# Causal scores in 64x64 array tiles, the state's products moved ahead of them, and the work around them reordered, in a gated linear attention followed by a routed FFN

## The chip, the cores and the metric

One core of a Trainium2 chip runs the whole program. The metric is device time in microseconds of one launch; smaller is better. The engines are PE (matmul) with its weight loads PEld, DVE (vector), ACT (scalar), POOL (GpSimd) and SP, which here only issues DMAs. SP issues to the hardware DMA queue, POOL issues the indirect (gather and scatter) DMAs to the software queue.

## The reference

All data is float32. Attention has batch B=4, H=8 heads, S=768 steps, head size D=48; its result becomes the rows x of an FFN with E=8 experts of which each row takes its two best.

```python
f = 1 / (1 + exp(-f_logit))
for t in range(S):
    state = f[:, :, t, :, None] * state + einsum('bhd,bhe->bhde', k[:, :, t], v[:, :, t])
    y[:, :, t] = einsum('bhd,bhde->bhe', q[:, :, t], state)
x = y as (B*S, H*D) = (3072, 384)
noisy = x @ w_gate + log1p(exp(x @ w_noise)) * noise
top2, weights = two largest of noisy, softmax over the two
out[row] = sum over the two e of weight_e * (relu(x[row] @ w1[e]) @ w2[e])    # w1: 384x1024, w2: 1024x384
```

## The kernel before

**Steps.** The attention is cut into 24 steps: n = c*B + b, with c one of 6 chunks of C=128 time steps and b the batch. A step handles all 8 heads, as HP=4 pairs (`hp`); the two heads of a pair (`par`) lie on partitions 0 to 63 and 64 to 127, each padded from 48 to DP=64.

**Stages of a step.** `forget` transposes f on PE and takes its log on ACT. `summed` is a running sum on DVE (a tensor-tensor scan, L554). `decays` makes P and Q, two exponentials of the sum, on ACT. `scaled` transposes q and k on PE; DVE multiplies them into qP (L566) and kQ (L568). `scores` transposes kQ back (kp, L574; not in the last chunk), multiplies kQ by qP on PE into a two-bank PSUM tile `sc` (L580), and DVE multiplies that by the lower-triangle mask `causal` into A (L583). `output` multiplies A by v on PE (y, L598), makes the state's increment ds from kn and v (L604), adds the state's part, state by qP, to y (L609; not in the first chunk), has ACT copy y (yT, L613) and ds (dss, L618) out of PSUM, and POOL computes the new state from dss, the old state and P (mid L625, st L626). `features` multiplies yT by a constant matrix (xp, L633) that brings x into row order and gives the router's logits; ACT copies the rows (xs, L638), which SP stores to `x_rows` in DRAM at the next `scaled` (L639).

**Order.** An outer loop over i runs from -3 to 25. In each pass every stage handles its own step n = i - lag, in a written order; between the stages small pieces of other work are dropped in. `slot` counts the stages run. From the line `first` on, each engine's instructions keep the order in which they are traced. In the last passes, stages that have run out of steps are left out.

**Loads.** `load` (L528) brings f, q, k and v of a step, 192 KB each, in one DMA of 192-byte runs. They go into rings of 5, 4, 4 and 6 buffers. POOL clamps f two passes ahead of its use (L534); for the first three steps DVE does it.

**Routing.** After every fourth step `route(c)` works out the two experts of a chunk's rows, one small group of instructions a slot. Its end gives 8 `put`s: each a scatter by POOL (L710) of 128 list entries to the `lists` tensor in DRAM, and a small memset (L719). One put is issued every third slot.

**The FFN's beginning.** When the puts of the first three chunks (24 of them) have been issued, the generator `first_loads` begins: after some slots SP fetches the first list (`slots<-lists`, L815), POOL gathers the rows that it names (`xg<-x_rows`, L826, in two halves), and PE transposes them (`turned`, xgp, L862). After that, pieces of expert 0's first layer (hp, L914) are put between the last stages of the attention. The rest of the FFN follows as one stream, most of it matmuls of L914, L939 and L1021.

**Zeros.** `out` is first filled with zeros, since the FFN's results are added to it: 24 DMAs of 192 KB on SP (L1254), twelve of them one at a time at the outputs of steps 5 to 16, twelve in the FFN. `lists` is filled from the tile `empty` at step 5 (L1309). SP also issues the first experts' weights in parts of 384 KB (L841, L844), from step 17 on.

**PSUM.** Six banks (`one_bank`) are taken in turn by all products but the scores.

Of the kernel before, what the change touches and what calls it, by code (L numbers as in the profile page):

```python
# [10 lines left out]
F32 = mybir.dt.float32  # L11
# [320 lines left out]
def kernel(  # L332
# [89 lines left out]
        turns.append(turns.pop(0))  # L422
        return turns[-1].tile([128, 512], F32, tag="one", name=name)

    def two_banks(name):
        return ps2.tile([128, 2, 512], F32, tag="two", name=name)


    ident = const.tile([128, 128], F32, tag="ident", name="ident")
# [23 lines left out]
    def counting(name, pattern, base=0, by_partition=0):  # L453
# [9 lines left out]
    over_of = counting("over_of", [[QS, NI]], base=3 * 256)  # L463
    block = counting("block", [[1, NI]])

    causal = const.tile([128, 128], F32, tag="causal", name="causal")
    nc.gpsimd.affine_select(out=causal, in_=ones, compare_op=ALU.is_ge, fill=0.0, base=0,
                            pattern=[[1, 128]], channel_multiplier=-1)
# [5 lines left out]
    LR = E * N + 256  # L474
    x_rows = tc.dram_tile([N, DM], F32, name="x_rows")
    lists = tc.dram_tile([LR, 4], U32, name="lists")
    empty = const.tile([128, LR // 128, 4], U32, tag="empty", name="empty")

    cap = [const.tile([128, HP, C], F32, tag=f"cap{i}", name=f"cap{i}") for i in range(2)]
    for i in range(2):  # L480
# [44 lines left out]
    def load(nm, n):  # L525
        c, b = n // B, n % B
        if n < NCH * B:
            nc.sync.dma_start(out=pads[nm][n % RING[nm]][:, :, 0:D],  # L528
                              in_={"f": f_logit, "q": q, "k": k, "v": v}[nm][b, :, c * C:(c + 1) * C, :].rearrange("h t d -> t h d"))

    def clamp(n, engine=nc.gpsimd):
        if n < NCH * B:
# [31 lines left out]
    def scaled(n):  # L564
        qP[n] = wk.tile([128, HP * C], F32, tag="qP", name=f"qP_{n}", bufs=3)
        nc.vector.tensor_tensor(qP[n], transposed("q", n), P[n], ALU.mult)  # L566
        kQ[n] = wk.tile([128, HP * C], F32, tag="kQ", name=f"kQ_{n}")
        nc.vector.tensor_tensor(kQ[n], transposed("k", n), Q[n], ALU.mult)  # L568

    def scores(n):  # L570
        if n // B < NCH - 1:
            kp = one_bank(f"kp_{n}")
            for hp in range(HP):
                nc.tensor.transpose(kp[:, cols(hp)], kQ[n][:, cols(hp)], ident)  # L574
            kn[n] = wk.tile([C, H, DP], F32, tag="kn", name=f"kn_{n}")
            nc.scalar.copy(kn[n].rearrange("t h d -> t (h d)"), kp)
        sc = two_banks(f"sc_{n}")
        for hp in range(HP):
            for par in range(2):
                nc.tensor.matmul(sc[:, par, cols(hp)], lhsT=kQ[n][rows(par), cols(hp)],  # L580
                                 rhs=qP[n][rows(par), cols(hp)], start=True, stop=True)
        A[n] = wk.tile([C, 2, HP * C], F32, tag="A", name=f"A_{n}")
        nc.vector.tensor_tensor(A[n].rearrange("j r (a i) -> j (r a) i", i=C), sc.rearrange("j r (a i) -> j (r a) i", i=C),  # L583
                                causal.unsqueeze(1).broadcast_to((C, H, C)), ALU.mult)

    def output(n):
        c, b = n // B, n % B
        vt = pads["v"][n % RING["v"]]


        y = [one_bank(f"y{odd}_{n}") for odd in range(2)]

        def at(hp, par):
            return y[hp % 2][rows(par ^ hp % 2), cols(hp // 2)]

        for hp in range(HP):
            for par in range(2):
                nc.tensor.matmul(at(hp, par), lhsT=vt[:, 2 * hp + par, :], rhs=A[n][:, par, cols(hp)],  # L598
                                 start=(hp < 2), stop=(c == 0 and hp >= HP - 2))
        if c < NCH - 1:  # L600
            ds = one_bank(f"ds_{n}")
            for hp in range(HP):
                for par in range(2):
                    nc.tensor.matmul(ds[rows(par), hp * DP:(hp + 1) * DP], lhsT=kn[n][:, 2 * hp + par, :],  # L604
                                     rhs=vt[:, 2 * hp + par, :], start=True, stop=True)
        if c:
            for hp in range(HP):
                for par in range(2):
                    nc.tensor.matmul(at(hp, par), lhsT=state[b][rows(par), hp, :],  # L609
                                     rhs=qP[n][rows(par), cols(hp)], start=False, stop=(hp >= HP - 2))  # L610
        yT[n] = wk.tile([128, 2, HP // 2 * C], F32, tag="yT", name=f"yT_{n}")
        for odd in range(2):
            nc.scalar.copy(yT[n][:, odd, :], y[odd][:, 0:HP // 2 * C])  # L613
        if c == NCH - 1:
            return

        dsv = wk.tile([128, HP, DP], F32, tag="ds", name=f"dss_{n}")
        nc.scalar.copy(dsv, ds[:, 0:HP * DP].rearrange("d (a e) -> d a e", e=DP))  # L618
        end = P[n].rearrange("d (a t) -> d a t", t=C)[:, :, C - 1:C].broadcast_to((128, HP, DP))
        new = wk.tile([128, HP, DP], F32, tag=f"st{b}", name=f"st_{n}")  # L620
        if c == 0:
            nc.gpsimd.tensor_tensor(new, dsv, end, ALU.mult)
        else:
            mid = wk.tile([128, HP, DP], F32, tag="mid", name=f"mid_{n}")
            nc.gpsimd.tensor_tensor(mid, dsv, state[b], ALU.add)  # L625
            nc.gpsimd.tensor_tensor(new, mid, end, ALU.mult)  # L626
        state[b] = new
# [631 lines left out]
    def first_loads():  # L1259
        while n_routed < HALF or len(n_put) < HALF * B * 2:  # L1260
            yield
        for _ in range(3):
            yield
        for what, p, pause in (("fetch", 1, 5), ("first", 0, 3), ("second", 0, 1), ("fetch", 2, 4), ("turned", 0, 0),
                               ("first", 1, 3), ("second", 1, 1), ("fetch", 3, 1)):
            if what == "fetch":
                ahead(what, p)
            elif what == "first":
                gather(p, (0,))
            elif what == "second":  # L1270
# [12 lines left out]
    slot = n_routed = n_first = 0  # L1283
    pieces = chain.from_iterable(((k, i) for i, _ in enumerate(first_layer(k) if k < NE else first_of_two(k))) for k in range(len(items)))
    for i in range(-3, NS + 2):
        for stage, lag in ((forget, -3), (scaled, -1), (scores, 0), (summed, -2), (output, 1), (decays, -2), (features, 2)):
            n = i - lag
            if not 0 <= n < NS:
                continue
# [128 lines left out]
```

## Time and profile before

| | us |
|---|---|
| median of 3 runs (657.47 to 659.05) | 657.95 |
| profiled execution: its own time | 658.33 |
| profiled execution: its span | 656.6 |
| busy in the span: PE / DVE / POOL / ACT | 635.6 / 442.6 / 272.6 / 254.0 |
| one pass in the middle of the attention (score products at 61.6, then 67.62) | 6.0 |
| first score product of step 0 / of step 22 | 12.76 / 138.84 |
| first piece of expert 0 | 149.27 |

The span runs from the first to the last instruction; 1.7 us of the execution lie outside of it. The last steps of the attention lie among the first pieces of expert 0 and end at about 170 us. A record of a matmul lasts longer than the array is taken by it, since the records overlap; what a group costs PE is read from the start of one group to the start of the next. Each matmul of these float32 operands has two records, so the 8 score products of a step are 16.

### The profile page before, as it was taken

The page shows a single profiled execution, that of the slowest core. Times are in us where ns is not written, and L with a number is a line of the kernel's source. Part 1 is how long each engine was busy: PE and PEld are TensorE (multiplying, and loading weights), DVE is VectorE, ACT ScalarE, POOL GpSimd, SP SyncE. Part 2 cuts the span into 40 slices and gives each one's busy share as a digit, 9 for nine tenths or more (in the row PEclk, how much of TensorE's full clock was granted, in tenths as well). Part 3 has the DMA queues.
Part 4 walks back from the last instruction along what each step waited for, and adds up shares of the span by engine and source line. Part 5 has one row for each costly group of instructions (what it writes and reads, how often), then busy time and mean ns, then how long its engine had stood idle before and what let it go on. Part 6 is the DMA issues. An engine that isn't in the chain of part 4 may idle for free.

```text
span 656.6 us, 12905 instructions
## 1 busy us (share of the span) xinstructions
PE 635.6 (97%) x4883; PEld 549.1 (84%) x4883; DVE 442.6 (67%) x993; ACT 254.0 (39%) x603; POOL 272.6 (42%) x300
## 2 busy tenths in 40 slices
PE   7999999979999999999999999999999999999991
PEld 7999999968999999989758965995698579889891
DVE  7777877854476577677657575666666666766751
ACT  5876776732222234233332233223332332232320
POOL 8633999853187531352502450334035114413021
PEclk9999999999999999999999999999999999999996
DMA  9999988982998423368707560925275246601122
GB/s 192 195 221 213 199 188 185 205 248 31 321 311 189 66 37 96 70 192 288 197 25 252 93 193 0 317 42 175 72 245 124 65 146 187 180 2 25 23 25 29
DMA packets 153897, 96.31 MB, mean 147 GB/s; under 512 B 115600, under 2 KB 146320, under 8 KB 153824
## 3 DMA queue, kind: packets, MB, share of 16 engines
q1 hardware_dynamic: 141648, 76.12, 42.1%
q0 software_dynamic: 12176, 19.25, 15.0%
q8 instruction: 41, 0.67, 0.4%
q14 instruction: 32, 0.26, 0.1%
HBM read 75.97 MB, written 19.62 MB: 146 GB/s over the span
## 4 chain that ended last, share of the span: by engine, by line
PE 92%; DMA 4%; DVE 1%; POOL 1%; issue 1%; SPq 0%; POOLq 0%; DVEq 0%
PE y L1021 32%; PE P L939 8%; PE hp L914 6%; PE W L939 5%; PE Z L939 5%; PE V L939 5%; PE X L939 5%; PE y L598 4%; PE xp L633 3%; PE sc L580 3%; PE xgp L862 2%; PE y L609 2%; PE fp L540 1%; PE kp L540 1%; PE ds L604 1%; PE kp L574 1%
## 5 line engine op out<-in xcount | busy, mean ns | idle before, releaser
L1030 POOL DMA_INDIRECT out_dram<-ys,slots x48 | 81.2, 1691 | 178.1 <-ACT ys L1088 144.6
L1021 PE MATMUL y<-qk_all,f_all 128*128 128x192 f32 x576 | 105.2, 327 | 0.0
L1021 PEld LDWEIGHTS y<-qk_all,f_all 128*128 128x128 f32 x576 | 93.3, 190 | 0.3 <-DVE f_all L1003 0.3
L826 POOL DMA_INDIRECT xg<-x_rows,slots x48 | 54.2, 1130 | 19.9 <-issue 11.1
L710 POOL DMA_INDIRECT lists<-entry,sloti x48 | 55.4, 1153 | 10.6 <-issue 9.3
L1021 PE MATMUL y<-w,hs_b 128*128 128x192 f32 x320 | 59.1, 328 | 0.0
L1021 PEld LDWEIGHTS y<-w,hs_b 128*128 128x128 f32 x320 | 52.9, 190 | 0.9
L1162 POOL DMA_INDIRECT out_dram<-ys_q,slots_q x5 | 8.6, 1713 | 104.6 <-DVE ys_q L1160 104.6
L914 PE MATMUL hp<-xt_a,w 128*128 128x256 f32 x192 | 43.7, 382 | 0.0
L975 ACT ACTIVATE hs_b<-hs_b 128x256 f32<-128x256 f32 (+1 forms) x32 | 15.1, 470 | 71.7 <-DVE hs_b L955 71.7
L914 PEld LDWEIGHTS hp<-xt_a,w 128*128 128x128 f32 x192 | 35.8, 190 | 4.8 <-issue 0.2
L939 PE MATMUL X<-xt_a,w 128*128 128x256 f32 (+1 forms) x128 | 39.7, 432 | 0.0
L939 PE MATMUL Z<-xt_b,v_all 128*128 128x256 f32 (+1 forms) x128 | 39.7, 432 | 0.0
L1080 DVE TENSOR_TENSOR ys<-P,y 128x192 f32<-128x192 f32 x24 | 8.5, 354 | 43.1 <-PE y L1021 29.8
L583 DVE TENSOR_TENSOR A<-sc,causal 128x1024 f32<-128x1024 f32 x24 | 29.3, 1222 | 10.0 <-PE sc L580 9.1
L1088 ACT ACTIVATE ys<-ys,slots 128x384 f32<-128x384 f32 x24 | 14.8, 615 | 55.1 <-DVE ys L1087 55.1
L955 DVE TENSOR_TENSOR hs_b<-hs_a,X 128x256 f32<-128x256 f32 (+1 forms) x32 | 15.6, 487 | 29.9 <-PE X L939 29.8
L1021 PE MATMUL y<-w,f_all 128*128 128x192 f32 x192 | 35.1, 326 | 0.0
L939 PEld LDWEIGHTS Z<-xt_b,v_all 128*128 128x128 f32 x128 | 24.3, 190 | 10.1
L939 PEld LDWEIGHTS X<-xt_a,w 128*128 128x128 f32 x128 | 24.3, 190 | 10.1
L955 DVE TENSOR_TENSOR hs_a<-hs_a,P 128x256 f32<-128x256 f32 (+1 forms) x64 | 31.1, 485 | 1.5
L1021 PEld LDWEIGHTS y<-w,f_all 128*128 128x128 f32 x192 | 31.9, 190 | 0.0
(199 smaller groups left out, 1437.4 us busy)
## 6 DMA issues: line engine op xcount, KB each, us to landing
w<-in_moe_w_dram SPq DMA_DIRECT2D x16, 1536.0 KB, 8.5
w_q<-in_moe_w_dram SPq DMA_DIRECT2D x10, 1536.0 KB
w<-in_moe_w_dram SPq DMA_DIRECT2D x16, 384.0 KB, 5.3
f_all<-in_f_logit_dram SPq DMA_DIRECT2D x24, 192.0 KB, 3.4
qk_all<-in_q_dram SPq DMA_DIRECT2D x24, 192.0 KB, 4.5
qk_all<-in_k_dram SPq DMA_DIRECT2D x24, 192.0 KB, 4.6
v_all<-in_v_dram SPq DMA_DIRECT2D x24, 192.0 KB, 5.3
x_rows<-xs SPq DMA_DIRECT2D x24, 192.0 KB, 5.8
```

The lines of the kernel that those rows point to most:

```text
L580: nc.tensor.matmul(sc[:, par, cols(hp)], lhsT=kQ[n][rows(par), cols(hp)], rhs=qP[n][rows(par), cols(hp)], start=True, stop=True)
L583: nc.vector.tensor_tensor(A[n].rearrange("j r (a i) -> j (r a) i", i=C), sc.rearrange("j r (a i) -> j (r a) i", i=C), causal.unsqueeze(1). ...
L598: nc.tensor.matmul(at(hp, par), lhsT=vt[:, 2 * hp + par, :], rhs=A[n][:, par, cols(hp)], start=(hp < 2), stop=(c == 0 and hp >= HP - 2))
L633: nc.tensor.matmul(xp[:, hp, :], lhsT=yT[n][:, hp % 2, cols(hp // 2)], rhs=w_rt[:, hp, :], start=True, stop=True)
L710: into = nc.gpsimd.indirect_dma_start(out=lists, out_offset=bass.IndirectOffsetOnAxis(ap=sloti[:, r, b:b + 1], axis=0), in_=entry[:, c, b, ...
L826: nc.gpsimd.indirect_dma_start(out=xg[p][:, s, :], out_offset=None, in_=x_rows[0:HALF * B * C] if p < NE else x_rows, in_offset=bass.Indir ...
L914: nc.tensor.matmul(hp[:, o, :], lhsT=w1[home(k)][:, i, (fo + o) * 128:(fo + o + 1) * 128], rhs=xt_a[:, i, k % 2 * 256:(k % 2 + 1) * 256], ...
L939: nc.tensor.matmul(to, lhsT=x, rhs=y, start=start, stop=stop)
L955: nc.vector.tensor_tensor(to, x, y, ALU.add)
L975: nc.scalar.activation(c(1, 1), c(1, 1), AF.Relu)
L1021: nc.tensor.matmul(P[name], lhsT=x[:, o, :], rhs=y[:, o, :], start=(o == 0), stop=(o == FH - 1))
L1030: into = nc.gpsimd.indirect_dma_start(out=out, out_offset=bass.IndirectOffsetOnAxis(ap=slots[p][:, s, 2:3], axis=0), in_=ys[s], in_offset= ...
```

## The change

It does nine things.

1. The scores go to one PSUM tile for the whole attention, `sc_all`, which DVE fills with zeros once at the start. Each pair's product is made in two parts: the earlier 64 rows of keys (T=64) with all 128 queries, and the later 64 with the later 64 queries. The quarter that the mask would clear is not written. A product now has 64 partitions of kQ, 64 columns of it, and 128 or 64 columns of qP: 16 matmuls a step instead of 8.
2. In heads 4 to 7 the two halves of the keys are swapped: kQ is written with them exchanged, so DVE makes kQ in two instructions; v of these heads is loaded likewise, so a load of v is three DMAs. The pairs are taken in the order 0, 2, 1, 3.
3. The mask `causal` is a tile of four pairs instead of one, made by six POOL instructions instead of one.
4. `empty` is half as large, and `lists` is filled from it in two DMAs.
5. The state's part of y (`from_state`) is issued in the next `scores`, between the kp transposes and the score products; it starts the accumulation, and A by v ends it.
6. `features` stands ahead of `decays` in a pass.
7. While the third chunk's routing is the last begun, a put is issued every second slot instead of every third.
8. `first_loads` waits 7 slots instead of 3; its later pauses are 4, 2, 1, 6 where they were 5, 3, 1, 4.
9. The attention's twelve zeros go out two at a time at the outputs of steps 17 to 22.

```diff
+    sc_all = ps2.tile([128, 2, 512], F32, tag="two", name="sc_all")
+    nc.vector.memset(sc_all, 0.0)
...
+    T = C // 2
+    causal = const.tile([128, HP, 128], F32, tag="causal", name="causal")
+    for hp in range(HP):
+        for base, n in ((0, 128),) if hp < HP // 2 else ((T, 128), (-T, T)):
+            nc.gpsimd.affine_select(out=causal[0:n, hp], in_=(causal[0:n, hp] if n == T else ones), ...
...
-    empty = const.tile([128, LR // 128, 4], U32, tag="empty", name="empty")
+    empty = const.tile([128, LR // 256, 4], U32, tag="empty", name="empty")
...
+            nc.sync.dma_start(out=to[:, 0:H // 2], in_=rows_in[0:H // 2].rearrange("h t d -> t h d"))
+            for half in range(2):
+                nc.sync.dma_start(out=to[half * T:(half + 1) * T, H // 2:],
+                                  in_=rows_in[H // 2:, (1 - half) * T:(2 - half) * T].rearrange("h t d -> t h d"))
...
-        nc.vector.tensor_tensor(kQ[n], transposed("k", n), Q[n], ALU.mult)
+        kt = transposed("k", n)
+        for far_ in range(2):
+            out_, x, y = (z.rearrange("d (o a s t) -> d o a s t", o=2, s=2, t=T)[:, far_] for z in (kQ[n], kt, Q[n]))
+            nc.vector.tensor_tensor(out_[:, :, ::-1, :] if far_ else out_, x, y, ALU.mult)
...
-        for hp in range(HP):
-            for par in range(2):
-                nc.tensor.matmul(sc[:, par, cols(hp)], lhsT=kQ[n][rows(par), cols(hp)],
-                                 rhs=qP[n][rows(par), cols(hp)], start=True, stop=True)
+        if n:
+            from_state(n - 1)
+        for hp in (0, 2, 1, 3):
+            for late_rows in range(2):
+                half = hp // 2 ^ late_rows
+                for par in range(2):
+                    nc.tensor.matmul(sc_all[half * T:(half + 1) * T, par, hp * C + late_rows * T:(hp + 1) * C],
+                                     lhsT=kQ[n][rows(par), hp * C + half * T:hp * C + (half + 1) * T],
+                                     rhs=qP[n][rows(par), hp * C + late_rows * T:(hp + 1) * C], start=True, stop=True)
...
+    def from_state(n):
+        y_of[n] = [one_bank(f"y{odd}_{n}") for odd in range(2)]
+        if n // B:
+            for hp in range(HP):
+                for par in range(2):
+                    nc.tensor.matmul(place(n, hp, par), lhsT=state[n % B][rows(par), hp, :],
+                                     rhs=qP[n][rows(par), cols(hp)], start=(hp < 2), stop=False)
...
-        for _ in range(3):
+        for _ in range(7):
             yield
-        for what, p, pause in (("fetch", 1, 5), ("first", 0, 3), ("second", 0, 1), ("fetch", 2, 4), ("turned", 0, 0),
+        for what, p, pause in (("fetch", 1, 4), ("first", 0, 2), ("second", 0, 1), ("fetch", 2, 6), ("turned", 0, 0),
...
-        for stage, lag in ((forget, -3), (scaled, -1), (scores, 0), (summed, -2), (output, 1), (decays, -2), (features, 2)):
+        for stage, lag in ((forget, -3), (scaled, -1), (scores, 0), (summed, -2), (output, 1), (features, 2), (decays, -2)):
...
-                    nc.sync.dma_start(out=lists.rearrange("(p r) w -> p r w", p=128), in_=empty)
+                    for part in range(2):
+                        nc.sync.dma_start(out=lists.rearrange("(g p r) w -> g p r w", g=2, p=128)[part], in_=empty)
...
-                if 5 <= n < 5 + NS // 2:
-                    zeros(1)
+                if 17 <= n < 17 + NS // 4:
+                    zeros(2)
...
-            if puts and slot % 3 == 0:
+            if puts and slot % (2 if n_routed == HALF else 3) == 0:
```

More of the change, by code (lines that the diff above doesn't have):

```diff
@@ L423, in one_bank @@
         return turns[-1].tile([128, 512], F32, tag="one", name=name)
-    def two_banks(name):
-        return ps2.tile([128, 2, 512], F32, tag="two", name=name)
+    sc_all = ps2.tile([128, 2, 512], F32, tag="two", name="sc_all")
+    nc.vector.memset(sc_all, 0.0)
     ident = const.tile([128, 128], F32, tag="ident", name="ident")
@@ L464 @@
     block = counting("block", [[1, NI]])
-    causal = const.tile([128, 128], F32, tag="causal", name="causal")
-    nc.gpsimd.affine_select(out=causal, in_=ones, compare_op=ALU.is_ge, fill=0.0, base=0,
-                            pattern=[[1, 128]], channel_multiplier=-1)
+    T = C // 2
+    causal = const.tile([128, HP, 128], F32, tag="causal", name="causal")
+    for hp in range(HP):
+        for base, n in ((0, 128),) if hp < HP // 2 else ((T, 128), (-T, T)):
+            nc.gpsimd.affine_select(out=causal[0:n, hp], in_=(causal[0:n, hp] if n == T else ones), compare_op=ALU.is_ge, fill=0.0,
+                                    base=base, pattern=[[1, 128]], channel_multiplier=-1)
     earlier = const.tile([128, 128], F32, tag="earlier", name="earlier")
@@ L527, in load @@
         if n < NCH * B:
-            nc.sync.dma_start(out=pads[nm][n % RING[nm]][:, :, 0:D],
-                              in_={"f": f_logit, "q": q, "k": k, "v": v}[nm][b, :, c * C:(c + 1) * C, :].rearrange("h t d -> t h d"))
+            to = pads[nm][n % RING[nm]][:, :, 0:D]
+            rows_in = {"f": f_logit, "q": q, "k": k, "v": v}[nm][b, :, c * C:(c + 1) * C, :]
+            if nm != "v":
+                nc.sync.dma_start(out=to, in_=rows_in.rearrange("h t d -> t h d"))
+                return
+            nc.sync.dma_start(out=to[:, 0:H // 2], in_=rows_in[0:H // 2].rearrange("h t d -> t h d"))
+            for half in range(2):
+                nc.sync.dma_start(out=to[half * T:(half + 1) * T, H // 2:],
+                                  in_=rows_in[H // 2:, (1 - half) * T:(2 - half) * T].rearrange("h t d -> t h d"))
     def clamp(n, engine=nc.gpsimd):
@@ L576, in scores, with place @@
             nc.scalar.copy(kn[n].rearrange("t h d -> t (h d)"), kp)
-        sc = two_banks(f"sc_{n}")
-        for hp in range(HP):
-            for par in range(2):
-                nc.tensor.matmul(sc[:, par, cols(hp)], lhsT=kQ[n][rows(par), cols(hp)],
-                                 rhs=qP[n][rows(par), cols(hp)], start=True, stop=True)
-        A[n] = wk.tile([C, 2, HP * C], F32, tag="A", name=f"A_{n}")
-        nc.vector.tensor_tensor(A[n].rearrange("j r (a i) -> j (r a) i", i=C), sc.rearrange("j r (a i) -> j (r a) i", i=C),
-                                causal.unsqueeze(1).broadcast_to((C, H, C)), ALU.mult)
+        if n:
[7 more added lines that the diff above has]
+                                     rhs=qP[n][rows(par), hp * C + late_rows * T:(hp + 1) * C], start=True, stop=True)
+        A[n] = wk.tile([C, 2, HP * C], F32, tag="A", name=f"A_{n}")
+        nc.vector.tensor_tensor(A[n], sc_all, causal.rearrange("j a i -> j (a i)").unsqueeze(1).broadcast_to((C, 2, HP * C)), ALU.mult)
+    y_of = {}
+    def place(n, hp, par):
+        return y_of[n][hp % 2][rows(par ^ hp % 2), cols(hp // 2)]
+    def from_state(n):
[5 more added lines that the diff above has]
+                                     rhs=qP[n][rows(par), cols(hp)], start=(hp < 2), stop=False)
     def output(n):
@@ L588, in output @@
         vt = pads["v"][n % RING["v"]]
-        y = [one_bank(f"y{odd}_{n}") for odd in range(2)]
-        def at(hp, par):
-            return y[hp % 2][rows(par ^ hp % 2), cols(hp // 2)]
+        if n not in y_of:
+            from_state(n)
+        y = y_of[n]
         for hp in range(HP):
             for par in range(2):
-                nc.tensor.matmul(at(hp, par), lhsT=vt[:, 2 * hp + par, :], rhs=A[n][:, par, cols(hp)],
-                                 start=(hp < 2), stop=(c == 0 and hp >= HP - 2))
+                nc.tensor.matmul(place(n, hp, par), lhsT=vt[:, 2 * hp + par, :], rhs=A[n][:, par, cols(hp)],
+                                 start=(c == 0 and hp < 2), stop=(hp >= HP - 2))
         if c < NCH - 1:
@@ L605, in output @@
                                      rhs=vt[:, 2 * hp + par, :], start=True, stop=True)
[L606 to L610, printed above, removed]
         yT[n] = wk.tile([128, 2, HP // 2 * C], F32, tag="yT", name=f"yT_{n}")
```

## The prediction

> **What bounds the kernel now.** I read the page first, then the groups by line, PE's and POOL's timelines in the attention, the waits and the chain.
>
> The page's slices and the chain, shares by engine:
>
> ```profile
> PE   7999999979999999999999999999999999999991
> POOL 8633999853187531352502450334035114413021
> ...
> PE 92%; DMA 4%; DVE 1%; POOL 1%; issue 1%; SPq 0%; POOLq 0%; DVEq 0%
> ```
>
> PE is full but for the start and the ninth slice; POOL is full in slices 5 to 7, about 66 to 115 us. PE's timeline, one pass:
>
> ```profile
> 66.65 0.60 PE L540 MATMUL kp<-ident,qk_all 128*128 128x128 f32 x4
> 67.09 0.60 PE L574 MATMUL kp<-ident,kQ 128*128 128x128 f32 x4
> 67.62 1.16 PE L580 MATMUL sc<-qP,kQ 64*128 64x128 f32 x16
> 68.71 1.09 PE L598 MATMUL y<-A,v_all 128*64 128x128 f32 x16
> 69.63 0.64 PE L604 MATMUL ds<-v_all,kn 128*64 128x64 f32 x16
> 70.20 0.67 PE L609 MATMUL y<-qP,st 64*64 64x128 f32 x16
> 70.80 1.15 PE L633 MATMUL xp<-w_rt,yT 128*128 128x112 f32 x8
> ```
>
> From start to start: scores 1.09, y 0.92, ds 0.57, state 0.60, xp 0.98; with 1.84 for the four transposes 6.0 us a pass, without idle time: PE sets the pace. The ninth slice, in the chain of waits from 126 us:
>
> ```profile
> 128.97 6.08 DMA lists<-entry,sloti
> ...
> 135.06 1.73 DMA slots<-lists
> ...
> 137.61 6.70 DMA xg<-x_rows,slots
> ...
> 144.35 0.79 PE xgp L862 x3
> 145.13 1.91 PE y L598 x16
> ```
>
> PE finishes the scores of step 22 at 139.95 and waits in front of xgp for the gathered rows until 144.35; by the windows its clock is then at half for 3.4 us (0.53 in 144.35 to 148.00). The loss is 4.35 + 1.7 us. The chain starts at the 24th put. When does POOL issue that?
>
> ```profile
> 125.58 1.68 POOL L710 DMA_INDIRECT lists<-entry,sloti  x1 [0.22 <-issue]
> 127.27 0.09 POOL L719 MEMSET spacer<- 1x1 f32 x1
> 127.32 0.73 POOL L625 TENSOR_TENSOR mid<-dss,st 128x256 f32<-128x256 f32 x1
> 128.13 0.68 POOL L626 TENSOR_TENSOR st<-mid,P 128x256 f32<-128x256 f32 x1
> 128.97 1.01 POOL L710 DMA_INDIRECT lists<-entry,sloti  x1 [0.16 <-issue]
> ```
>
> POOL has no gap over 0.3 us before it; from 66 to 130 us it is busy 58.9 of 64 us and the rest is 0.15 to 0.2 us ahead of each put. Put 16, traced at the scores of step 16 (104.2), runs at 108.88. So POOL is behind its order of work, and the 24th put goes out when POOL's work is done. After 145 us PE has no idle time: what the attention gains or loses reaches the end.
>
> **What the Trainium skill says.** "TensorEngine Tiling (Array Packing)", Tiling Modes: 64x64 gives four tiles that work independently, and a change of mode drains the array. The trace agrees with both: the records of the state's products (64x64) start four together every 0.109 us, and around each change of shape 0.15 to 0.2 us are lost. The same page, Performance Considerations, says that a matmul has about 60 cycles of overhead and one column costs as much as 60; ds (64 columns) starts a pair every 0.058 us against 0.109 for 128, so 64 columns still pay half here. "GPSIMD Engine Reference", Specifications: POOL shares its SBUF port with DVE's instructions of two SBUF inputs. The puts that meet DVE's scan take 1.7 to 1.9 us instead of 1.0 (that at 125.58, scan from 125.28 to 126.49). "DMA: Bandwidth & Descriptors", SWDGE vs HWDGE vs iDMA: an engine takes turns between the software and the hardware queue; no view here shows the shares.
>
> **The change, part by part.**
>
> *Scores.* Before: 8 pairs of records, every 0.111 us: 0.89. After, each of the four tiles gets four records of 128 and four of 64 columns, and the order 0, 2, 1, 3 gives both column halves the same. 128 columns cost 0.109 (state). A 64x64 product of 64 columns is not in the trace: between 0.058 (ds) and 0.109; I take ds. 4 x 0.109 + 4 x 0.058 = 0.67 (to 0.87): gain 0.22 (0.02 to 0.22).
>
> *State ahead.* Shapes run full, scores, y/ds, state, full: four changes. Leftovers from the records: into scores 0.19, scores to y 0.15, ds to state 0.15, state to xp 0.18. After: full to state 0.15, none to the scores, 0.15, 0.18. Gain 0.19, in steps with a state. A pass then takes 6.0 - 0.41 = 5.6 us.
>
> *Start.* DVE's zeroing of 1024 columns: six memsets of 128 columns take 0.87 us at 4.63, so 1.16. DVE idles 0.59 before its first clamp, which the chain runs through: +0.5 (0 to 1.2). POOL makes five more masks (0.25 each) and four memsets half as long (-0.7): its first clamp, 7.94 to 9.74, moves by 0.4, and its reader starts at 10.81: nothing.
>
> *DVE.* kQ in two instructions: +0.1 a pass (128x512 takes 0.68, 128x256 about 0.42). A stays 1024 wide. DVE is busy 51.8 of 64 us and waits for the scores (7.2 us in 14 waits); that covers it.
>
> *Loads.* v adds two issues of 0.4 us a step to SP, a zero less saves 0.5 to 0.7; bytes stay. v is loaded three steps ahead, so nothing. The second DMA of `lists`: 0.4 us of SP once, at step 5, long before the first put.
>
> *Features ahead of decays.* On ACT the rows' copy (0.49) goes before P and Q; but y is now complete after A by v and its copy no longer waits for ds and the state (1.1 us), so P is not later. The copy also frees the bank that y takes earlier. Cost nothing.
>
> *The 24th put.* POOL's full stretch begins with the state update of step 8, at 65.9, which waits for dss. Up to there PE gains 5 x 0.22 + 5 x 0.41 - 0.5 = 2.65, counted at xp (64.79 to 62.1); y and ds end there, dss ends at 62.75 instead of 65.8, the update starts at 62.8. POOL's work from there to the 24th put is 63.1 us. The update of step 18 falls behind the put (-1.65), and a shorter pass puts one more scan in the way (+0.7). So 62.8 + 63.1 - 1.65 + 0.7 = **124.9**, 4.1 earlier. Every second slot brings nothing: POOL is late already. It also ends up further behind PE: st of step 16 ends at 116.87 and P of step 20, which takes its buffer (four), starts at 121.0; that margin of 4 us goes, and ACT may wait up to 2 us at steps 16 to 19. PE's following idle time covers that.
>
> *The rows.* From put to rows 15.4 us: 124.9 + 15.4 = **140.3**. The later fetch (7 slots) reaches SP near 123 and still waits for the puts.
>
> *PE's arrival.* xp in the pass of step 21, 136.89, moves to 129.3 (2.65 + 12 x 0.41). Then xp 0.98, transposes 0.97, state 0.44, scores 0.82 with the change of shape, y of step 21 0.92: PE stands before xgp at 133.5 and idles 6.8 us. The clock halves as before.
>
> *Sum.* The rows come 4.05 earlier; y and state of step 21, 0.92 + 0.60, are done ahead of the wait instead of behind it; step 23 gains 0.41. Total **-6.0 us**. The profiled execution (658.33, span 656.6 and 1.7 around it) becomes 652.3; it stands 0.4 over the median, 657.95, so I forecast **652.0**. A measurement tells 0.3%, 2 us, from no change.
>
> **Rivals.**
>
> *The chain is shorter than I add it up, and the wait goes.* For it: puts take 1.0 us without a scan, the packets of the puts at 119.47 and 124.26 were through 3.3 us later against 5.5 for the 24th, and without zeros at steps 5 to 16 the queues are emptier. Then PE's own gain shows: 7.6 + 0.41 + 0.41 (steps to 21, 22, 23) and the 6.05 us of the stall: 643.5; half of it 648. Against: POOL's work does not shrink with DMA traffic.
>
> *The zeros take the gather's place.* Ten zeros are issued before the rows arrive; 128 packets of 1536 bytes at 67 ns over 16 engines are 0.54 us each, 5.4 us. If all of it lies in the chain: 657.4, no change. Against: SP, stuck on the fetch, leaves the queues empty; DMA's share was 0.64 from 130 to 140.
>
> *Slower: the column halves take turns.* Place: the score products. The scores now run only two tiles at a time, and a row pair shares its columns; if that stays so, 8 x 0.109 + 8 x (0.058 to 0.109) = 1.34 to 1.74 instead of 0.89. Over 22 steps, less the change of shape, PE arrives 7 to 16 us later, the wait is gone, and the end is 1.3 to 10.8 later: 659 to 669, 664 in the middle. It decides from a score block of 1.3 us. Against: the state's products start four at a time.
>
> That the change doesn't do what it says I see no way for, except the put rate, dealt with above.
>
> **How the numbers follow.** Forecast 0.53 (649 to 655 by itself: the chain 3 us shorter or longer); wait gone or halved 0.22; zeros in the way 0.12; slower 0.13. Faster: 0.53 + 0.22 + 0.05 of the zeros' case = 0.80; same 0.07; slower 0.13. The range leaves out the slower case and the end of the fastest: 645.0 to 657.5.
>
> **What would show it.** Score groups 0.7 to 0.8 us from start to start with four records together; passes of 5.6 us; the 24th put near 125, rows near 140, PE idle 6 to 7 us before xgp, with POOL again without gaps. Wrong if PE does not wait there, if a score block is over 1.1 us, or if put to rows is not 14 to 17 us.

## The result, and the profile after

The changed kernel takes **677.59 us** (675.14 to 678.51) against 658.5 us for the kernel before beside it: a ratio of 1.0281, 95% interval 1.0245 to 1.0317. The forecast was 652.0. The profiled execution has a span of 676.2 us, 19.6 more than before. Every ratio here is taken over fast executions alone, so it is not quite the quotient of the medians beside it (in the second group below, where the kernel before scattered from 664 to 680 us, the two differ by up to 0.8%).

The page's slices of the kernel after, in tenths of busy time (the granted clock in the third line, the DMA engines' share in the fourth):

```profile
PE   8999988963999999999999999999999999999990
POOL 7544677816047634151441351235034214413021
PEclk9999998995999999999999999999999999999996
DMA  9887777799199533264753761646093337602112
```

Where PE had only the ninth slice short of full, it now has gaps from the sixth slice on and almost stands still in the tenth. POOL is nowhere full in slices 4 to 7. The DMA share falls there to 0.7 to 0.8; by the windows from 62 to 122 us it is 0.77 after and 0.90 before, at 151 and 198 GB/s. PE, POOL and the DMA engines all do less per us: something else must hold them back.

PE's own part came out as planned. PE's timeline, one undisturbed pass:

```profile
68.29 0.67 PE L612 MATMUL y<-qP,st 64*64 64x128 f32 x16
68.78 0.85 PE L596 MATMUL sc_all<-qP,kQ 64*64 64x128 f32 x32
69.55 1.09 PE L625 MATMUL y<-A,v_all 128*64 128x128 f32 x16
```

State 0.49, scores 0.77 from start to start; passes 5 to 8 start 5.57 us apart. But from the scores of step 9 (63.0) to those of step 17 (117.8) a pass takes 6.85 us, 6.16 before. The chain of waits shows through what (start, us, what):

```profile
81.59 4.64 DMA x_rows<-xs
...
89.61 4.69 DMA x_rows<-xs
...
95.69 7.53 DMA x_rows<-xs
...
150.83 4.23 DMA slots<-lists
...
158.61 6.48 DMA xg<-x_rows,slots
...
165.22 0.87 PE xgp L884 x3
```

Stores of rows, which the chain of before did not hold, stand in it from step 12 to step 15. ACT's timeline says how (in brackets the idle time ahead of an instruction and what ended it):

```profile
94.37 0.48 ACT L660 COPY xs<-xp 128x384 f32<-128x384 f32 x1 [3.75 <-DMA x_rows<-xs]
94.75 0.63 ACT L569 ACTIVATE P<-L 128x512 f32<-128x512 f32 x1
95.28 0.62 ACT L571 ACTIVATE Q<-L 128x512 f32<-128x512 f32 x1
```

xs has three buffers. Its copy waits until the store of three steps ago has landed, and P and Q of a later step stand behind it on ACT; DVE then waits for P (18.8 us in 17 waits from 12 to 175 us). Why are the stores late? The queue that issues them, SP's timeline:

```profile
83.51 1.00 SPq L536 DMA_DIRECT2D v_all<-in_v_dram  x1
84.56 1.27 SPq L538 DMA_DIRECT2D v_all<-in_v_dram  x2
85.88 0.61 SPq L508 DMA_DIRECT2D noise<-in_moe_noise_dram  x1
86.59 0.44 SPq L534 DMA_DIRECT2D f_all<-in_f_logit_dram  x1
87.13 0.53 SPq L534 DMA_DIRECT2D qk_all<-in_q_dram  x1
87.76 1.76 SPq L534 DMA_DIRECT2D qk_all<-in_k_dram  x1
89.61 1.89 SPq L661 DMA_DIRECT2D x_rows<-xs  x1
91.54 0.43 SPq L536 DMA_DIRECT2D v_all<-in_v_dram  x1
```

SP has no gap much over 0.1 us; the store at 89.61 lies behind all the loads. v's two half loads (L538) take 1.27 us together in nearly every step. Adding up SP's issues from the scores of step 9 to those of step 17 gives 5.62 us of 6.16 a step before and 6.34 of 6.85 after. This share says little: it is 88 to 97% in every kernel traced here, since the same kind of issue lasts longer in some places than in others. What tells is how late SP is. Here are a copy of rows and its store, and a load of k and its first use on PE, first before, then after (the 24 of each are matched in order):

```profile
66.83 0.50 ACT L638 COPY xs<-xp 128x384 f32<-128x384 f32 x1
...
70.40 0.59 SPq L639 DMA_DIRECT2D x_rows<-xs  x1
...
93.55 2.25 SPq L528 DMA_DIRECT2D qk_all<-in_k_dram  x1
...
109.96 0.60 PE L540 MATMUL kp<-ident,qk_all 128*128 128x128 f32 x4
```

```profile
80.56 0.48 ACT L660 COPY xs<-xp 128x384 f32<-128x384 f32 x1 [2.39 <-DVE lg L658]
...
95.69 1.34 SPq L661 DMA_DIRECT2D x_rows<-xs  x1
```

The load of k at 87.76, above, is used here, and PE waits for it:

```profile
93.55 0.63 PE L550 MATMUL kp<-ident,qk_all 128*128 128x128 f32 x4 [0.33 <-DMA qk_all<-in_k_dram]
```

From step 9 to 17 a store follows the end of its copy by 2.6 to 4.7 us before and by 12.4 to 16.7 after, so these stores do not wait for their copies: SP is some 10 us, about a step and a half, later than before. And k is loaded 15.1 to 16.8 us ahead of its use before, 5.8 to 8.1 after: the three steps of look-ahead are almost gone.

The fetch of the slots, in front of the FFN, is late too. First SP before the change, then after it, around the first fetch of the slots:

```profile
129.12 0.41 SPq L639 DMA_DIRECT2D x_rows<-xs  x1
135.06 0.37 SPq L815 DMA_DIRECT2D slots<-lists  x1
```

```profile
148.81 1.27 SPq L538 DMA_DIRECT2D v_all<-in_v_dram  x2
150.13 0.60 SPq L863 DMA_DIRECT2D w<-in_moe_w_dram  x1
150.83 0.43 SPq L837 DMA_DIRECT2D slots<-lists  x1
151.30 0.94 SPq L1276 DMA_DIRECT2D out_dram<-zero  x2
```

Before, SP stood idle from 129.5 until the 24th put had landed. After, that put is issued at 131.77, and SP comes to the fetch only 19.06 us later, straight from other issues. (The change's longer pauses make little of this: in s1_v_act below, with the same pauses but an SP that keeps up, the fetch comes 8.0 us after the put.) The sum of the loss, after less before:

- 24th put 131.77 against 128.97: **+2.8**
- put to fetch 19.06 against 6.09: **+13.0**
- fetch to gather 5.14 against 2.55: +2.6 (two zeros follow the fetch; but without zeros there, in e2_zeros_early below, it was 4.2)
- gather to the rows in front of xgp 5.97 against 6.74: -0.8
- xgp to the first product of the FFN 6.43 against 4.92: +1.5 (after PE's idle time the clock is at half for longer than before, and other products stand between; the two are not separated)

Together 19.1 of the 19.6 us; the FFN behind it lasts 507.8 us, 507.3 before.

### The profile page after: what moved, and what is told of

Read it like the earlier page. It is cut to its first block, busy times and chain, and to the rows that moved or that the text cites. A ratio compares the mean times of both kernels' runs of the same rounds, so it can differ in the third digit from the quotient of the medians.

```text
span 676.2 us, 13746 instructions
## 1 busy us (share of the span) xinstructions
PE 635.3 (94%) x5267; PEld 550.9 (81%) x5267; DVE 447.7 (66%) x1018; ACT 253.7 (38%) x603; POOL 264.5 (39%) x305
## 3 DMA queue, kind: packets, MB, share of 16 engines
q0 software_dynamic: 12176, 19.25, 14.6%
## 4 chain that ended last, share of the span: by engine, by line
PE 80%; DVE 7%; DMA 5%; ACT 4%; issue 2%; POOL 1%; SPq 0%; POOLq 0%; DVEq 0%; ACTq 0%
PE y L1043 31%; PE P L961 8%; PE hp L936 6%; PE Z L961 5%; PE V L961 5%; PE X L961 5%; PE W L961 5%; DMA x_rows<-xs 2%; PE xgp L884 2%; DVE L L564 2%; PE xp L655 2%; PE y L625 1%; PE sc_all L596 1%; DVE A L600 1%; PE yp_q L1178 1%
## 5 line engine op out<-in xcount | busy, mean ns | idle before, releaser
L848 POOL DMA_INDIRECT xg<-x_rows,slots x48 | 52.7, 1098 | 54.7 <-DMA slots<-lists 24.1
L732 POOL DMA_INDIRECT lists<-entry,sloti x48 | 50.7, 1056 | 12.0 <-issue 9.5
L997 ACT ACTIVATE hs_b<-hs_b 128x256 f32<-128x256 f32 (+1 forms) x32 | 15.1, 470 | 71.7 <-DVE hs_b L977 71.7
L884 PE MATMUL xgp<-ident,xg 128*128 128x128 f32 x144 | 24.3, 279 | 14.9 <-DMA xg<-x_rows,slots 14.9
L1110 ACT ACTIVATE ys<-ys,slots 128x384 f32<-128x384 f32 x24 | 14.8, 615 | 57.6 <-DVE ys L1109 55.8
L977 DVE TENSOR_TENSOR hs_b<-hs_a,X 128x256 f32<-128x256 f32 (+1 forms) x32 | 15.6, 486 | 30.0 <-PE X L961 29.8
L576 DVE TENSOR_TENSOR qP<-qp,P 128x512 f32<-128x512 f32 x24 | 16.6, 692 | 23.8 <-ACT P L569 18.8
L600 DVE TENSOR_TENSOR A<-sc_all,causal 128x1024 f32<-128x1024 f32 x24 | 29.2, 1217 | 4.7 <-PE sc_all L596 4.6
```

Source lines behind the costliest of these rows:

```text
L600: nc.vector.tensor_tensor(A[n], sc_all, causal.rearrange("j a i -> j (a i)").unsqueeze(1).broadcast_to((C, 2, HP * C)), ALU.mult)
L732: into = nc.gpsimd.indirect_dma_start(out=lists, out_offset=bass.IndirectOffsetOnAxis(ap=sloti[:, r, b:b + 1], axis=0), in_=entry[:, c, b, ...
L848: nc.gpsimd.indirect_dma_start(out=xg[p][:, s, :], out_offset=None, in_=x_rows[0:HALF * B * C] if p < NE else x_rows, in_offset=bass.Indir ...
L884: nc.tensor.transpose(xp[:, i * 128:(i + 1) * 128], xg[p][:, s, i * 128:(i + 1) * 128], ident)
L977: nc.vector.tensor_tensor(to, x, y, ALU.add)
L997: nc.scalar.activation(c(1, 1), c(1, 1), AF.Relu)
```

## The experiments

**Theories.** (a) v's split: SP, which issues in order and has no gaps before either, gets 1.2 us a step more, and all that is queued behind it comes late. (b) Features ahead of decays: P and Q stand behind xs on ACT. (c) The late zeros stand ahead of the fetch and the gather. (d) The start: DVE's zeroing delays the clock and the first scores. In the expectations SyncE, ScalarE and VectorE are SP, ACT and DVE.

The runs came in groups on different chips, on which the kernel before took 664 to 676 us. Ratios to before are best compared within a group; the changed kernel's own 1.0281 comes from another measurement, and where two groups are compared the text says so. Times of traces of different groups are not subtracted. Intervals are 95%.

### First group: one part of the change undone (before: 663.96 us)

**n1_no_swap**

```diff
-            if nm != "v":
+            if True:                       # v whole, one DMA
-        for far_ in range(2): ... kQ in two multiplies
+        nc.vector.tensor_tensor(kQ[n], transposed("k", n), Q[n], ALU.mult)
-                half = hp // 2 ^ late_rows
+                half = late_rows           # causal: ((0, 128),) for every pair
```

> The changed kernel without the swap: v in one DMA, kQ in one multiply, one causal mask for all heads; the scores stay in 64x64 tiles without the upper quarter, but now one output half does all the 128-column products (8 x 0.109 = 0.87 us instead of 0.67). SyncE's two issues more (v: 3 x 0.62 = 1.87 us a step after, 0.66 before) are gone. If SyncE's queue is what made the change slow (stores of x_rows late, the slots' fetch 19 us after the 24th put), the passes of steps 9 to 16 are 5.6 to 6.0 us without the stalls, the fetch goes out within 6 us of the 24th put, PE's wait in front of xgp is under 8 us instead of 14.2, and the time is 654 to 662. If the order features ahead of decays on ACT or the late zeros made it slow, the pass is 0.2 us longer and the rest stays: 676 to 682.

Measured 668.79, ratio **1.0078** (1.0051 to 1.0105), against 1.0281 with the swap: 2.0% come back (2.2 to 2.8% against the three other kernels of this group). From step 9 to 17 a pass takes 6.16 us; a store follows its copy by 1.5 to 4.4 us (10.8 to 18.4 in the three others), and k is loaded 12.8 to 17.0 us ahead (4.9 to 8.9). SP keeps up again. The fetch goes out 8.8 us after the put (137.20 after 128.36), and PE waits 7.9 us, in two parts, before xgp. The swap with its loads of v is the cause of most, but less came back than (a) expected: fetch within 6 us, and 654 to 662 us, which on a chip with 658 for the kernel before is -0.6 to +0.6%.

**e2_zeros_early**

```diff
-                if 17 <= n < 17 + NS // 4:
-                    zeros(2)
+                if 5 <= n < 5 + NS // 2:
+                    zeros(1)
```

> The changed kernel with the zeros back at one a step from step 5 to 16. If the late zeros are what delays the fetch and the gather, SyncE has two issues (1.2 us) a step less in steps 17 to 22, the fetch goes out about 8 us earlier and the time is 666 to 671. If v's issues on SyncE are the cause, the zeros' issue of 0.65 us a step only moves into steps 9 to 16, where SyncE is full already (6.3 of 6.9 us): stalls there grow by what is saved behind them, 674 to 682.

Measured 686.97, **1.0353** (1.0296 to 1.0409): no gain, rather a loss, at the upper end of the second case. The kernel's waits (us in all, times, longest) from 12 to 175 us:

```profile
ACT xs L660 <- DMA x_rows<-xs: 27.7, 9, 5.3
DVE qP L576 <- ACT P L569: 27.5, 15, 5.9
```

ACT now waits for the stores 27.7 us in 9 waits, 9.2 us in 3 with the late zeros: an issue put into the stretch where SP is late comes out as a wait on ACT and DVE. This speaks for (a), against (c).

**e3_decays_first**

```diff
-..., (output, 1), (features, 2), (decays, -2)):
+..., (output, 1), (decays, -2), (features, 2)):
```

> The changed kernel with decays ahead of features again. If P and Q waiting on ACT behind the rows' copy xs is the cause, DVE's waits for P (18.8 us in 17) fall to under 6 us, the passes of steps 9 to 16 return to 5.6 to 6.0 us and the time is 664 to 669. If SyncE's queue is the cause, xs still waits for the store of three steps before and the fetch still waits for SyncE: 674 to 678, with the first piece of the gathered rows where it was.

Measured 683.55, **1.0315** (1.0248 to 1.0382). Waits for P are no longer among the largest, as (b) has it, but a pass still takes 6.62 us from step 9 to 17 and the time is no better. PE's wait for the gathered rows is as long as ever:

```profile
PE xgp L884 <- DMA xg<-x_rows,slots: 13.8, 2, 12.6
```

So (b) names a symptom: with P moved off the late xs, PE still ends behind SP.

**e4_late_memset**

```diff
-    nc.vector.memset(sc_all, 0.0)          # ahead of everything
     clamp(1, nc.vector)
+    nc.vector.memset(sc_all, 0.0)
```

> The changed kernel with DVE's zeroing of the score banks after its second clamp instead of ahead of everything. The start loses what it had lost: clock full from about 5 us instead of 11.9, the first scores near 13 instead of 15.6. If SyncE's queue sets the order from step 9 on, of these 2.8 us under 1 us reaches the end: 676 to 678. If PE's own path or ACT's order sets it, all of it does: 674 to 675.5.

Measured 681.38, **1.0298** (1.0226 to 1.037): no gain, and the first scores moved by only 0.8 us, to 14.7. With the zeroing ahead of everything they came at 12.9 (n1), 13.4 (e2) and 14.8 (e3) on the same chip, so the start differs that much from one traced execution to the next. The start is not what made 2.8%, and that the memset makes the start late is not shown.

### Second group: v's loads by themselves (before: 674.57 us)

**b1_v_three**, the kernel before and one edit:

```diff
+            nc.sync.dma_start(out=to[:, 0:H // 2], in_=rows_in[0:H // 2]...)
+            for half in range(2):
+                nc.sync.dma_start(out=to[half * C // 2:(half + 1) * C // 2, H // 2:],
+                                  in_=rows_in[H // 2:, half * C // 2:(half + 1) * C // 2]...)
```

> The kernel before with nothing changed but v's load: three DMAs a step in the changed kernel's shapes (128 partitions x 4 heads, then 64 x 4 heads twice), rows where they belong. If v's issues on SyncE are the cause, SyncE needs 5.62 + 1.2 = 6.8 us a step in steps 9 to 16 against passes of 6.16 us: they stretch to 6.6 to 6.9, the fetch goes out over 8 us later, and the time is 2 to 3.5% above before. If the split matters only together with the new order on ACT, the late zeros or the new score tiles, this kernel stays within 0.7% of before.

Measured 694.89, **1.0252** (1.021 to 1.0294). Almost the whole of the change's loss, without any other part of it. A pass from step 9 to 17 takes 7.56 us with 7.01 of SP's issues; stores follow their copies by 12.4 to 19.6 us, k is loaded 5.6 to 7.9 us ahead; the fetch leaves 15.0 us after a put that is itself late. SP's timeline:

```profile
91.61 3.35 SPq L646 DMA_DIRECT2D x_rows<-xs  x1
95.02 0.43 SPq L533 DMA_DIRECT2D v_all<-in_v_dram  x1
95.50 1.27 SPq L535 DMA_DIRECT2D v_all<-in_v_dram  x2
96.81 0.60 SPq L1261 DMA_DIRECT2D out_dram<-zero  x1
```

**b2_v_three_full**, the same three issues and bytes with all 128 partitions:

```diff
+            for part in range(2):          # heads 4 and 5, then 6 and 7
+                nc.sync.dma_start(out=to[:, H // 2 + part * H // 4:H // 2 + (part + 1) * H // 4], ...)
```

> The same, but the three DMAs of v are 4, 2 and 2 heads of all 128 partitions: as many issues and bytes, no 64-partition transfer. The whole-half-heads DMA of 128 partitions took 0.43 us of SyncE, those of 64 partitions 0.63. If the number of DMAs costs, this kernel is as slow as the one with 64-partition halves, give or take 0.5%. If the 64-partition shape costs (longer issue, DMA engines poorly used: their share fell from 0.9 to 0.73), it is within 0.7% of before.

Measured 686.54, **1.0154** (1.0102 to 1.0206). Between the two: two more issues cost about 1.5%, the 64-partition shape another 1%. Most issues of 128 partitions x 2 heads take 0.47 to 0.50 us, those of 64 x 4 heads 0.61, for the same 48 KB. SP is late here too: stores 9.7 to 14.6 us behind their copies, k 6.3 to 9.7 us ahead.

**s1_v_act**, the changed kernel with v's halves from ACT's queue:

```diff
             for half in range(2):
-                nc.sync.dma_start(out=to[half * T:(half + 1) * T, H // 2:], ...)
+                nc.scalar.dma_start(out=to[half * T:(half + 1) * T, H // 2:], ...)
```

> The changed kernel with v's two 64-partition DMAs issued from ScalarE's queue, SyncE keeping one issue of v. If SyncE's own issue time is the cause (6.34 of 6.85 us a step), it is back at 5.1 us, the stalls of steps 9 to 16 go, the fetch follows the 24th put within 6 us, and the time is -0.5 to +1% of before. If it is the transfers' shape on the DMA engines, nothing is won: +2 to +3%. If ScalarE becomes the bound (1.2 us of issue a step ahead of P, Q and the copies), stalls move to it: +1.5 to +4%.

Measured 676.76, **1.0112** (1.0072 to 1.0153) with the same transfers, against 1.0281 for the changed kernel (another measurement) and 1.0252 for b1 beside it; just above the -0.5 to +1% of the first case. SP keeps up: stores leave at most 2.8 us after their copies, k is loaded 16.3 to 22.4 us ahead. It is at the fetch 8.0 us after the put (133.66):

```profile
141.00 0.50 SPq L863 DMA_DIRECT2D w<-in_moe_w_dram  x1
141.61 1.16 SPq L837 DMA_DIRECT2D slots<-lists  x1
```

On ACT most issues take 0.60 to 0.67 us, and two of them stand in the chain between the scores of steps 14 and 15:

```profile
99.78 0.67 ACTq L538
...
100.49 0.67 ACTq L538
```

So more than half of the loss comes from the place of these issues on SP. But a pass from step 9 to 17 still takes 6.68 us, so something else stretches it here. Whether the last 1% is ACT's issue time or the half transfers, this run does not separate (by the medians it is 0.3%).

**n2_no_swap_zb**: the no-swap kernel with the zeros at steps 5 to 16 (edit of e2_zeros_early).

> The no-swap kernel with the zeros back at steps 5 to 16. In the no-swap kernel 6.4 us passed from the fetch's issue to the gather (2.5 before), behind w's loads and the late zeros, and the fetch left 9 us after the 24th put. If the late zeros cause that, the rows come 4 to 8 us earlier and the time is 0 to -0.8% of before. If SyncE is too full for zeros in steps 5 to 16 also without v's split (5.73 of 6.16 us a step without them), it stays at +0.5 to +1%.

Measured 678.45, **1.0057** (1.0032 to 1.0081) against 1.0078: the place of the zeros makes no difference that the intervals hold apart, though they make SP later (stores 8.0 to 15.1 us behind their copies; a pass takes 6.52 us).

### Third group: PE's part alone (before: 676.10 us)

**n3_pe_only** is n2_no_swap_zb with more edits undone; the tiles, the state ahead and the two DMAs of `lists` are left:

```diff
-    nc.vector.memset(sc_all, 0.0)          # back after clamp(1), as in e4
-(features, 2), (decays, -2)
+(decays, -2), (features, 2)
-        for _ in range(7):                 # ("fetch", 1, 4), ("first", 0, 2), ..., ("fetch", 2, 6)
+        for _ in range(3):                 # ("fetch", 1, 5), ("first", 0, 3), ..., ("fetch", 2, 4)
-            if puts and slot % (2 if n_routed == HALF else 3) == 0:
+            if puts and slot % 3 == 0:
```

> Of the change only the 64x64 score tiles (unswapped, column halves unequal), the state's part ahead of them and the banks zeroed, here after the second clamp; zeros at steps 5 to 16, decays first, put rate and pauses as before. By PE's records the pass is about 5.8 us where nothing holds it up, 0.2 less than before. If what was left above before in the no-swap kernels (0.6 to 0.8%) came from features ahead of decays, the start or the put rate, this kernel is at -0.2 to -0.8% of before. If SyncE's queue (6.06 us a step) bounds the passes of steps 9 to 16 whatever PE saves, it stays at 0 to +0.7%.

Measured 674.78, **0.9987** (0.9956 to 1.0018): between the two cases, and no change that this measurement can tell from zero.

**n3f_features_first** is the same with features ahead of decays.

> The same with features ahead of decays, the only difference. If the order on ScalarE costs (P behind xs, which waits for VectorE's lg and for the store of three steps before), it is 0.4 to 1% slower than its twin; if the prediction was right that the order costs nothing, they agree within 0.2%.

Measured 673.30, **0.9967** (0.9944 to 0.999): level with its twin, so no cost of the order on ACT shows. Its PE timeline at the scores of step 5:

```profile
37.83 0.67 PE L608 MATMUL y<-qP,st 64*64 64x128 f32 x16
38.32 1.05 PE L592 MATMUL sc_all<-qP,kQ 64*64 64x128 f32 x32
39.30 1.09 PE L621 MATMUL y<-A,v_all 128*64 128x128 f32 x16
```

State and scores take 1.47 us, 1.69 before; passes of 5.8 us in steps 5 to 8 against 6.0. Of 0.2 us a pass, some 4 us in all, 0.33% or 2.2 us reach the end: from step 9 to 17 a pass takes 6.36 us, SP's stores are 8.1 to 13.0 us behind their copies, and the fetch leaves 8.1 us after the put. So SP is late at times without v's split too.

**n4_zeros_out** and **s4_swap_relieved**: n3_pe_only, and the changed kernel with decays first and the late memset, each with no zeros in the attention:

```diff
-                if 17 <= n < 17 + NS // 4:
-                    zeros(2)
-        if len(zeroed) < NS and item:
-            zeros(1)
+        if len(zeroed) < NS and (item or piece >= 4):
+            zeros(1 if item else 2)
```

> The 64x64-tiles-only kernel with the zeros taken out of the attention: twelve go out in the first block's pieces, two each. SyncE loses 0.65 us (192 KB) a step in steps 5 to 16. If SyncE's queue and the DMA engines are the bound there, passes are 5.8 us in steps 9 to 16, the fetch goes out within 6 us of the 24th put, and the time is 0.8 to 1.8% below before. If PE or POOL set the pace, it is as its twin with the zeros inside.

> The changed kernel, swap and v's three DMAs kept, with the zeros out of the attention, decays first and the zeroing of the banks after the second clamp. SyncE issues no zeros in steps 17 to 22 (1.2 us a step less), so the fetch goes out about 7 us earlier; steps 9 to 16 keep 6.3 us of SyncE against passes of 5.6. If v's issues are enough to sink the change, it stays at +1 to +2% of before; if late zeros or the order on ScalarE mattered as much, it is within 0.7% of before.

Measured 684.29, **1.0157** (1.0108 to 1.0206), and 695.6, **1.0287** (1.0239 to 1.0334). Only two (n4) and four (s4) of the first twelve zeros got ahead of the first block's scatter; the others follow it and clear rows that it had added to, and the FFN is held up, so these times say nothing on the attention. What the traces say of it: in s4 a pass from step 9 to 17 takes 7.49 us, with no zero in it, and stores are 12.9 to 18.1 us behind their copies. Zeros are not what makes SP late there; v's loads are still in the queue. In n4 a pass takes 6.64 us, no better than with the zeros inside on the same chip (n3f 6.36, n3 6.99). I had expected 5.8.

### Fourth group: one part put back into n3f_features_first (before: 665.08 us)

**r2_swap_alone**: the swap with v's three DMAs, two kQ multiplies and balanced tiles, as in the change.

> The kernel at 0.9967 of before (64x64 tiles unswapped, state ahead, features first, late zeroing, zeros at 5 to 16, put rate and pauses as before) with the swap and v's three DMAs put in. If v's DMAs on SyncE are the main cause, it is +2 to +3% of before, as the kernel before with v in three was (1.0252). If the swap hurts only with the other edits, it is within 0.7% of before; the balanced tiles save PE 0.2 us a pass.

Measured 686.60, **1.0311** (1.0284 to 1.0338). The chain of this kernel from 100 us (its first piece begins before that):

```profile
93.11 7.21 DMA qk_all<-in_k_dram
...
109.32 6.61 DMA qk_all<-in_k_dram
...
117.52 8.56 DMA qk_all<-in_k_dram
...
155.01 4.31 DMA x_rows<-xs
...
160.72 4.73 DMA slots<-lists
```

A pass takes 8.14 us from step 9 to 17. Here k's loads, written three steps ahead, leave SP only 4.2 to 8.7 us before their use; stores are 15.5 to 19.9 us behind their copies (1.7 to 14.3 in the three that follow).

**r4_early_memset** (memset ahead of everything), **r6_pauses** (7 slots and the later pauses, puts still every third slot) and **r3_zeros_late** (zeros at 17 to 22):

> The kernel at 0.9967 with the score banks zeroed by VectorE ahead of everything, the only difference. The first scores come 1 to 3 us later, from the ones' and the clock's delay. If the start is carried to the end: +0.1 to +0.4% more, 0.998 to 1.001. If SyncE's loads set when the steps run, it does not show: 0.996 to 0.998.

> The kernel at 0.9967 with the later and longer pauses of the first loads alone (fetch four slots later in SyncE's order). If SyncE is behind PE there, each slot later costs its share of a step (5.6 / 7 = 0.8 us), so the fetch goes out up to 3.2 us later and the rows with it: 1.000 to 1.004. If the fetch still waits for the puts, as the prediction had it, no difference: 0.996 to 0.998.

> The kernel at 0.9967 with the zeros at steps 17 to 22, two a step, the only difference. If the zeros take the place of the fetch and the gather on SyncE and the DMA engines, the rows come 4 to 8 us later and the time is 1.002 to 1.008. If taking them out of steps 5 to 16 wins as much there (0.65 us of SyncE a step) as they cost later, it stays at 0.994 to 0.999.

Measured 670.15, **1.0057** (1.0032 to 1.0081); 666.81, **1.0024** (0.9999 to 1.0049); 666.41, **1.0018** (0.9999 to 1.0036). Each lies 0.5 to 0.9% above n3f's 0.9967, but that was measured on another chip, and in r4's trace the first scores are at 13.3 us, no later than n3f's 13.6. So what each small edit costs is not settled; each is at most about 1%. The early memset came out slower than either of its cases, the pauses within the first of theirs, the late zeros between theirs. Within this group the swap stands 2.5 to 2.9% above the three.

**n6_swap_v_act**: r2_swap_alone with v's halves issued from ACT (edit of s1_v_act), beside a kernel before of 674.52 us.

> The kernel with the swap at 1.0311 of before (everything else undone but the tiles, the state ahead, features first), with v's two 64-partition DMAs issued from ScalarE's queue. The transfers are the same. If SyncE's issues cost, it falls to 0.99 to 1.005; if the transfers do, it stays over 1.02; if ScalarE's issue time takes over, 1.005 to 1.02.

Measured 682.55, **1.0104** (1.0054 to 1.0155) against 1.0311 on the other chip: about two thirds of the swap's loss go with the issues. It falls in the middle case, where ACT's issue time takes over; there is no trace of it to show that. A swap that costs SP nothing was not found, and a no-swap kernel with the zeros after the gathered rows was not measured.

## Why the prediction was wrong

- **Scores 0.67, passes of 5.6: right.** Scores with their change of shape 0.77 (0.82 forecast), passes 5.57 us where nothing holds them up.
- **Loads: the step that failed.** The prediction said "v is loaded three steps ahead, so nothing", at 0.4 us an issue. Look-ahead hid the latency of the loads only as long as the queue that issues them kept up. The sum that the prediction left out was SP's own: 5.62 us of issues in a step of 6.16 without a gap, plus two at 0.61, less a zero of 0.5 to 0.7, is 6.1 to 6.3 us, in a step that was to take 5.6; measured, 6.34. SP fell about a step and a half behind: k left it 5.8 to 8.1 us before its use instead of 15.1 to 16.8. b1_v_three shows this step alone at +2.5%, n1_no_swap its removal at -2.0%, s1_v_act that it is the place of the issues on SP for more than half. What stays open is why issues stretch, and so how much room SP really has. The half loads were 0.61 us and not 0.4. The Trainium skill's "DMA: Bandwidth & Descriptors", Rules for kernel authors, advises one 128-partition transfer over two to partition halves, since halves share the same engines; b1 agrees that such a split gains nothing, and with b2 it adds that the halves' shape costs 1%.
- **"The later fetch (7 slots) reaches SP near 123 and still waits for the puts": wrong for the same reason.** SP reached it at 150.83. Put to rows was 30.2 us, not 15.4: of the signs that the prediction named for being wrong, this one came.
- **24th put 124.9: measured 131.77.** Of the 6.9 us, 3.2 are lost before POOL's full stretch begins (the state update of step 8 at 66.0 instead of 62.8): the first scores came 2.8 us later than before (0.5 forecast), and not every pass up to there gained its 0.4. The other 3.6 lie in the stretch: POOL, "without gaps" in the forecast, idles 6.8 us in front of clamps of f, whose loads come late, and 2.7 in front of state updates.
- **DVE's slack: misread, without harm.** The 7.2 us in 14 waits for the scores belong to the stretch from 12 to 150 us; in the 64 us beside which they are set, from 66 to 130, it is 3.4 in 6. At 0.1 a pass, some 1 us in these ten passes, that still covers it.
- **Features ahead of decays, "cost nothing": not contradicted** (n3 against n3f, the same chip). In the profile after, the longest wait is on this edit's path, ACT's xs, and taking that for the cause would have been a mistake (e3).
- **The start: 2.8 us late, 0.5 forecast.** Scores of step 0 at 15.6 instead of 13.3. But kernels with the same early zeroing began anywhere from 12.9 to 14.8, so how much of it the zeroing makes, and how much reaches the end, is open.
- **Rivals.** The slower one was the wrong mechanism: the column halves do not take turns, the score block never neared 1.3 us. "Zeros in the gather's place" saw the right spot for the wrong reason: fetch to gather grew by 2.6 us, while 13.0 us passed ahead of the fetch, and the zeros moved back did not recover them (e2).

## What to carry to other kernels

Before adding a DMA, look whether the queue that is to issue it keeps up: how long after its data is ready does a store leave, and how long before its use does a load? Its share of busy time does not tell. Here a queue without gaps, whose stores were about 3 us behind their data, fell 12 us and more behind when it got two issues of 0.6 us a step; that the loads were written three steps ahead did not help. When the chain shows waits for stores or fetches, look at what the issuing queue does just ahead of them; if it has no gap there and is late, the wait that the page names may be a symptom. A faster stage also shortens the step in which the other queues must finish.

## What the runs showed of the hardware

- A load of v holds SP 0.43 us at the median with 128 partitions x 8 heads (before) and with 128 x 4 (after), 0.50 with 128 x 2 (b2) and 0.61 with 64 x 4 (after, b1): fewer bytes do not make it shorter. From ACT the last takes 0.63 at the median. Shape alone does not set it: loads of f, q and k, all 128 x 8, take 0.44, 0.53 and 0.98 at the median from 50 to 130 us in the kernel after.
- The same kind of issue can last much longer: in the kernel after k's loads 0.53 to 3.19 us, stores of rows 0.32 to 3.08. From step 9 to 17 the copies of these stores had ended 12 us or more earlier, so the copy is not what they wait for; what stretches them is not shown.
- Fewer bytes and more DMAs gave a lower DMA share (0.77 against 0.90) and a slower kernel: the mean capacity of the DMA engines was not what bound it.
- After 14.2 us of idle time in front of xgp, PE's clock was 0.50 from 152 to 162 us and 0.51 from 162 to 169; before, after 4.35 us of idle time, it was 0.53 from 144.35 to 148 and full from 152.
